# Grouped 1x1 convolution: a head of 136 columns in four pieces, the ring begun at column 104, and no unrolled tail

## The chip, the core and the metric

The kernel runs on one core of a Trainium2 chip. The metric is the device time of one execution in microseconds (us), as the median of several executions.

## The reference, cut to what matters

```python
H = W = 512; G = 4; Cg = 48; C = G * Cg; k = 1      # bf16
x: (1, H, W, C);  w: (k, k, G, Cg, Cg)
xg = x.reshape(B, H, W, G, Cg)
out = einsum('bhwgc,gcd->bhwgd', xg, w[0, 0])       # k = 1: no neighbours, no padding
return out.reshape(B, H, W, C)
```

Each of the 262,144 pixels has 192 channels in four groups of 48; each group is multiplied by its own 48x48 matrix. 100.66 MB are read and as much is written.

## The kernel before, in words

**Columns, groups, pairs.** A pixel's 192 channels are contiguous in memory. On the chip 128 pixels stand in 128 partitions; one such set is a *column* (384 bytes a partition). Four columns are a *group* (196.6 KB), two groups a *pair*. There are 2056 columns, 514 groups and 257 pairs. A group takes 12 steps on TensorE: six transposes (L350), which bring channels to the partitions, and six matmuls against the block-diagonal weights `wt` (L370). VectorE copies a pair's transposes from PSUM to SBUF (L409), ScalarE (ACT) casts a group's result from PSUM to SBUF (L446).

**Fields.** `plan_fields` cuts the columns into *fields*. In a full field every partition holds one contiguous run of pixels. Two fields of 48 columns are *partial*: they use 120 partitions and go in several DMAs, two on the hardware queue (SP for loads, ACT for stores) and three on POOL's queue (L296, L307; with tiny "fill" DMAs between them, L286). Each is followed by a field of 32 columns, and the two together fill one slot of the ring.

**The load ring.** `ring` has 240 columns in three slots of 80 (`BIG`). `plan_pieces` cuts full fields into loads of 80 columns, the first ones into those of `HEAD`. `Piece.at` is the place in the ring: here four times the group's number, modulo 240. SP issues the loads in order (L320); `freed(p)` says how many pairs must have been transposed (`t_done`) before a load may overwrite its place, which is 60 groups before its end.

**The store ring.** `oring` has 280 columns. `plan_stores` cuts the fields into stores: mostly at the grid `OGRID` (72, 140, 212, 280), and in the last field's last 240 columns into smaller ones. ACT walks through all 514 groups in a straight program. Ahead of the cast of group g it issues every store that ended before g-1, and then waits for the landing of the store that last used the place of group g:

```python
while todo and stores[todo[0]].g1 <= g - 1:
    issue(todo.pop(0))          # L442, DMA at L427
if over[g] is not None:
    landed(over[g])             # waits for the older store in this place
act.copy(out_columns(g)..., o_ps[...])   # L446
```

The PSUM result buffer `o_ps` holds two groups, so TensorE waits soon after ACT does.

**TensorE's program.** `step(pair)` transposes pair+1 and then multiplies pair. `plan_units` puts pieces together to *units* of 80 columns that fill a slot ("regular"); TensorE waits for a unit's load at its first group (L344), for a mixed unit (partial field plus 32 columns) for a semaphore that POOL raises when all its parts have landed (L299, L300). `loop_spans` finds the run of regular units, and how many rounds of 60 groups (30 pairs, the period of the ring) fit into it. Before: pairs 0 to 8 unrolled, 8 rounds of 30 pairs (9 to 248), pairs 249 to 256 unrolled. Loads of irregular units have semaphores of their own.

The stores and pieces around the end, before (columns, groups from and up to):

| store | columns | groups | place in oring |
|---|---|---|---|
| 21 | 72 | 350-368 | 0 |
| 22 | 48 | 368-380 | 72 |
| 23 (partial) | 48 | 380-392 | 120 |
| 24 | 32 | 392-400 | 168 |
| 25 | 80 | 400-420 | 200 |
| 26 | 72 | 420-438 | 0 |
| 27 | 68 | 438-455 | 72 |
| 28, 29, 30 | 40 each | 455-485 | 140, 180, 220 |
| 31 to 36 | 20, 28, 24, 20, 16, 8 | 485-514 | 260, then 0 on |

Of the kernel before, what the change touches and what calls it, by code (L numbers as in the profile page):

```python
# [24 lines left out]
BIG = 80  # L25
SLOTS = 3
RCOLS = SLOTS * BIG
OGRID = (72, 140, 212, 280)
OCOLS = OGRID[-1]
HEAD = (8, 24, 48)  # L30
LATE_COLS = 240
LATE_PART = 40
LAST_PARTS = (24, 20, 16, 8)
# [13 lines left out]

FILL_ROWS = 5
FILL_BEFORE = (2, 3)


class Field:


    def __init__(self, cols, blocks, g0, pix):
        self.cols, self.g0, self.g1 = cols, g0, g0 + cols // 4
        self.full = blocks is FULL
        self.blocks = []
        for (queue, r0, rows, outer, less) in blocks:
            self.blocks.append((queue, r0, rows, outer, pix, cols - less))  # L60
            pix += rows * (cols - less)
        self.pix_end = pix
        assert cols % 4 == 0


class Piece:

    def __init__(self, i, field, c0, size):
        self.i, self.field = i, field
        self.c0, self.c1, self.size = c0, c0 + size, size  # L70
        self.g0, self.g1 = field.g0 + self.c0 // 4, field.g0 + self.c1 // 4
        self.at = 4 * self.g0 % RCOLS
        self.full, self.blocks = field.full, field.blocks
        assert size % 4 == 0 and self.at + size <= RCOLS

# [8 lines left out]
def plan_fields(npix):  # L84

    parts, head = [], sum(HEAD)
    for slots, special in FRONT:
# [14 lines left out]
def plan_pieces(fields):  # L102
    pieces = []
    for f in fields:
        first = [f.cols]
        if f.full:
            first = list(HEAD) if not f.g0 and sum(HEAD) <= f.cols else []
        c = 0
        while c < f.cols:
            n = first.pop(0) if first else min(BIG, f.cols - c)  # L110
            pieces.append(Piece(len(pieces), f, c, n))
            c += n
    return pieces
# [27 lines left out]
class Unit:  # L141


    def __init__(self, pieces):
        self.pieces, self.g0, self.g1 = pieces, pieces[0].g0, pieces[-1].g1
        self.slot = pieces[0].at // BIG
        self.regular = pieces[0].at % BIG == 0 and 4 * (self.g1 - self.g0) == BIG


def plan_units(pieces):  # L150
    units, rest = [], list(pieces)
    while rest:
        n = 1
        if rest[0].g0 and rest[0].at % BIG == 0:
            while n < len(rest) and rest[n].at % BIG:
                n += 1
        units.append(Unit(rest[:n]))
        rest = rest[n:]
    return units
# [19 lines left out]
def bass_standalone__grouped__vision_kernel(nc, x, w, out):  # L179
# [6 lines left out]
    pieces = plan_pieces(fields)  # L186
    stores = plan_stores(fields)
    units = plan_units(pieces)
    unit_of = {g: u for u in units for g in range(u.g0, u.g1)}
    store_of = {g: s for s in stores for g in range(s.g0, s.g1)}  # L190
# [12 lines left out]
    def transfers(ap, tile, part, queues):  # L203
        f, c0, c1, at = part.field, part.c0, part.c1, part.at
        for n, (queue, r0, rows, outer, pix, cols) in enumerate(f.blocks):
            if queue not in queues:
                continue
            px = ap[pix:pix + rows * cols, :]
            if f.full:
                view = px.rearrange("(p i) n -> p (i n)", p=rows)[:, c0 * C:c1 * C]  # L210
            else:
                assert (c0, c1) == (0, f.cols)
                view = px.rearrange("(c a i) n -> a c (i n)", a=outer, c=rows // outer)
            yield n, view, tile[r0:r0 + rows, at * C:(at + (c1 - c0 if f.full else cols)) * C]
# [12 lines left out]
    with ExitStack() as es:  # L227
# [25 lines left out]
        fill_sem = [sem(f"fill{k}") for k in range(4 * len(mixed))]  # L253

        def columns(g):
            at = 4 * g % RCOLS
            return ring[:, at * C:(at + 4) * C]

        def out_columns(g):
# [9 lines left out]
        def _(gp):  # L269
# [12 lines left out]
            def filler():  # L282
                k = len(used)
                src = xf[0:2 * FILL_ROWS, 0:4].rearrange("(t p) n -> p t n", t=2)
                dst = fill[:, 8 * k:8 * k + 8].rearrange("p (t n) -> p t n", t=2)
                gp.dma_start(dst, src).then_inc(fill_sem[k], 16)  # L286
                used.append(k)

            for nth, u in enumerate(mixed):
                part = [p for p in u.pieces if not p.full]  # L290
                for p in part:
                    gp.wait_ge(t_done, freed(p))
                    for n, dram, sbuf in transfers(xf, ring, p, ("pool",)):
                        if n in FILL_BEFORE:
                            filler()
# [6 lines left out]
                for i, s in enumerate(stores):  # L302
                    if any(s.field is p.field for p in part):
                        for n, dram, sbuf in transfers(of, oring, s, ("pool",)):
                            if n in FILL_BEFORE:
                                filler()
# [16 lines left out]
        def _(pe):  # L323
# [12 lines left out]
            def transposes(pair):  # L336
                todo = []
                for g in groups(pair):
                    u = unit_of[g]
                    if g % 2 and pair:  # L340
                        pe.wait_ge(e_done[(pair - 1) % NTOK], 1)
                    if g == u.g0:
                        for key in unit_keys[u]:
                            pe.wait_ge(ld_sem[key], 16)  # L344
                        todo += unit_keys[u] if u.regular else []
                    xg = columns(g)
                    for ul in range(2):
                        for tc in range(3):
                            j = ul * 3 + tc
                            last = pe.transpose(xT_ps[:, g % NXP, j * 128:(j + 1) * 128],  # L350
                                                xg[:, j * 128:(j + 1) * 128], ident[:])
                            if todo and 0 < j < 5:
                                last.then_inc(ld_sem[todo.pop(0)], -16)
                assert not todo
                last.then_inc(t_done, 1)
# [125 lines left out]
```

## Time and profile before

| | |
|---|---|
| median of 8 runs | 478.5 us (477.38 to 482.52) |
| profiled execution | 477.61 us, of which span 475.8 us |
| moved by DMA | 201.57 MB, 424 GB/s over the span |
| busy: PE, weight loads, ACT, DVE | 430.9, 389.1, 388.4, 246.8 us |
| TensorE clock, mean granted | 0.974 |
| ACT idle, of it waiting for a store to land | 81.7 us, 19.7 us in 10 waits |
| last load issued, landed | 410.6 us, 434.6 us |
| last cast begins, last store issued | 470.05 us, 470.88 us |

The span runs from the first to the last instruction on the core. Loads are on queue q1 (SP), stores on q10 (ACT), POOL's DMAs on q0. A DMA's row gives the time from its issue to its landing, which includes its time behind others in the queue.

### The profile page before, as it was taken

How to read it: one execution, taken by the hardware profiler on the slowest of the kernel's cores; microseconds unless marked ns; L12 is line 12 of the kernel's file. 1: busy time of each engine (PE TensorE's matmuls, PEld its weight loads, DVE VectorE, ACT ScalarE, POOL GpSimd, SP SyncE). 2: the span in 40 equal slices, each digit the busy share in tenths (PEclk: the TensorE clock that was granted, in tenths of full speed). 3: DMA queues.
4: the chain of work that ended last, by engine and by line, in shares of the span. 5: the costliest groups of instructions: out<-in, count | busy, mean ns of one | idle time of the engine just before them, and what ended most of it. 6: DMA issues, size and time to landing. Idle time of an engine off the chain costs nothing.

```text
span 475.8 us, 13580 instructions
## 1 busy us (share of the span) xinstructions
PE 430.9 (91%) x6178; PEld 389.1 (82%) x6178; DVE 246.8 (52%) x258; ACT 388.4 (82%) x515; POOL 12.5 (3%) x28
## 2 busy tenths in 40 slices
PE   5999999999598999999998997899978998997994
PEld 5888888888597988888987896788867987886883
DVE  2655556555255555555554554455535554653552
ACT  2998899988477898999986886789858987885885
POOL 1000000200002000000000000200002000000000
PEclk9999999999889999999998999999989999997998
DMA  8999999999999999999999999999999999999997
GB/s 329 444 394 427 424 426 430 436 426 434 437 428 429 433 425 429 438 432 425 431 438 433 429 437 420 435 426 439 428 429 429 434 430 426 432 431 433 422 408 310
DMA packets 10674, 201.57 MB, mean 424 GB/s; under 512 B 2112, under 2 KB 2112, under 8 KB 2752
## 3 DMA queue, kind: packets, MB, share of 16 engines
q1 hardware_dynamic: 4320, 97.44, 48.0%
q10 hardware_dynamic: 5120, 97.42, 47.9%
q0 software_dynamic: 1216, 6.49, 3.3%
q8 instruction: 9, 0.15, 0.1%
q14 instruction: 9, 0.07, 0.0%
HBM read 100.68 MB, written 100.66 MB: 423 GB/s over the span
## 4 chain that ended last, share of the span: by engine, by line
DMA 50%; PE 40%; ACT 7%; issue 1%; ACTq 1%; SPq 0%; POOLq 0%
DMA out_dram<-oring 40%; PE o_ps L370 23%; PE xT_ps L350 17%; DMA ring<-in_x_dram 9%; ACT oring L446 7%; ACTq L427 1%; SPq L320 0%; SPq L313 0%; ACTq L420 0%; POOLq L300 0%; POOLq L299 0%; ACTq L429 0%
## 5 line engine op out<-in xcount | busy, mean ns | idle before, releaser
L446 ACT CAST oring<-o_ps 128x768 bf16<-128x768 f32 x514 | 387.1, 801 | 81.7 <-PE o_ps L370 56.0
L409 DVE COPY xT_sb<-xT_ps 128x1536 bf16<-128x1536 bf16 x257 | 246.1, 958 | 218.0 <-PE xT_ps L350 218.0
L370 PE MATMUL o_ps<-wt,xT_sb 128*128 128x144 bf16 (+1 forms) x3084 | 288.9, 236 | 27.9 <-ACT oring L446 22.2
L370 PEld LDWEIGHTS o_ps<-wt,xT_sb 128*128 128x128 bf16 x3084 | 212.4, 99 | 66.5 <-ACT oring L446 57.4
L350 PE MATMUL xT_ps<-ident,ring 128*128 128x128 bf16 x3084 | 222.1, 222 | 8.2 <-POOLq L300 4.9
L350 PEld LDWEIGHTS xT_ps<-ident,ring 128*128 128x128 bf16 x3084 | 189.9, 100 | 11.2 <-POOLq L300 5.1
L286 POOL DMA_DIRECT2D fill<-in_x_dram x8 | 4.6, 573 | 351.1 <-PE xT_ps L350 230.6
L296 POOL DMA_DIRECT2D ring<-in_x_dram x6 | 3.3, 560 | 0.0
L307 POOL DMA_DIRECT2D out_dram<-oring x6 | 3.3, 556 | 0.0
L332 PE MATMUL o_ps<-w_sb,esel 48*128 48x48 bf16 x10 | 0.6, 209 | 2.6 <-DMA w_sb<-in_w_dram 2.6
L332 PEld LDWEIGHTS o_ps<-w_sb,esel 48*128 48x128 bf16 x10 | 0.4, 111 | 2.6 <-POOL esel L273 2.6
L402 DVE CAST wt<-o_ps 128x480 bf16<-128x480 f32 x1 | 0.7, 658 | 3.2 <-PE o_ps L332 3.2
L446 ACT ACT_TABLE_LOAD x1 | 1.3, 1283 | 0.8 <-PEq L466 0.8
L273 POOL TENSOR_SCALAR_AFFINE_SELECT esel<-esel 48x272 bf16<-48x272 bf16 x1 | 0.4, 402 | 0.0
L270 POOL MEMSET esel<- 48x272 bf16 x1 | 0.3, 318 | 0.3 <-POOLq L466 0.3
L277 POOL TENSOR_SCALAR_AFFINE_SELECT ident<-ident 128x128 bf16<-128x128 bf16 x1 | 0.3, 282 | 0.0
L271 POOL MEMSET ident<- 128x128 bf16 x1 | 0.2, 198 | 0.0
L466 POOL MEMSET const-float32-0.0<- 128x1 f32 x1 | 0.1, 99 | 0.3 <-issue 0.3
L466 POOL MEMSET const-bfloat16-1.0<- 128x1 bf16 x1 | 0.1, 102 | 0.0
L466 POOL MEMSET const-uint8-127<- 128x1 uint8 x1 | 0.1, 102 | 0.0
L466 POOL MEMSET const-float32-1.0<- 128x1 f32 x1 | 0.1, 99 | 0.0
## 6 DMA issues: line engine op xcount, KB each, us to landing
ring<-in_x_dram SPq DMA_DIRECT2D x22, 3840.0 KB, 26.2
out_dram<-oring ACTq DMA_DIRECT2D x11, 3456.0 KB, 39.7
out_dram<-oring ACTq DMA_DIRECT2D x10, 3264.0 KB, 39.9
out_dram<-oring ACTq DMA_DIRECT2D x3, 1920.0 KB, 18.2
out_dram<-oring ACTq DMA_DIRECT2D x1, 3840.0 KB, 46.3
ring<-in_x_dram SPq DMA_DIRECT2D x2, 1536.0 KB, 33.1
out_dram<-oring ACTq DMA_DIRECT2D x2, 1536.0 KB, 41.9
out_dram<-oring ACTq DMA_DIRECT2D x1, 2880.0 KB, 37.5
```

Source lines behind the costliest of these rows:

```text
L273: gp.affine_select(out=esel[:], in_=esel[:], pattern=[[-1, ECOLS]], compare_op=AluOpType.is_equal, fill=0.0, base=ESHIFT, channel_multipli ...
L286: gp.dma_start(dst, src).then_inc(fill_sem[k], 16)
L296: gp.dma_start(sbuf, dram).then_inc(ld_sem[ld_key[p.i, n]], 16)
L307: gp.dma_start(dram, sbuf).then_inc(st_sem[i][n], 16)
L332: last = pe.matmul(o_ps[:, NOB - 1, col:col + CG], lhsT=esel[:, s0:s0 + 128], rhs=w_sb[:, g, :], start=True, stop=True, skip_group_check=True)
L350: last = pe.transpose(xT_ps[:, g % NXP, j * 128:(j + 1) * 128], xg[:, j * 128:(j + 1) * 128], ident[:])
L370: last = pe.matmul(o_ps[:, v % NOB, c0_:c1_], lhsT=xs[:, j * 128:(j + 1) * 128], rhs=wt[:, WOFF[tc]:WOFF[tc] + (c1_ - c0_)], start=(tc == ...
L402: dve.tensor_copy(wt[:], o_ps[:, NOB - 1, 0:WCOLS]).then_inc(wc_sem, 1)
L409: dve.tensor_copy(xT_sb[pair % NXS][:, 0:n * 2 * UC].rearrange("p (g c) -> p g c", g=n), xT_ps[:, b0:b0 + n, 0:2 * UC]).then_inc(e_done[pa ...
L427: act.dma_start(dram, sbuf).then_inc(st_sem[i][n], 16)
L446: act.copy(out_columns(g).rearrange("p (u c) -> p u c", u=2), o_ps[:, v % NOB:v % NOB + 2, 0:UC]).then_inc(fa_done[g % (2 * NTOK)] if g < ...
L466: nc = _bacc.Bacc("TRN2", target_bir_lowering=False, num_devices=1)
```

## The change: what it does

`HEAD` becomes (8, 24, 48, 56), 136 columns in four loads. `ring_at` shifts all places in the ring by the head: the head begins at column 104 and ends at 240, and the 80-column units begin at column 0 behind it. The head's 56 columns are kept out of the regular units (`g0 > 0`, and `plan_units` merges only behind the head). Group numbers and places of the output are given by the same rules as before, so these follow:

- The first field has 616 instead of 560 columns, the last one 400 instead of 456. The partial fields are groups 154 to 165 and 394 to 405 instead of 140 to 151 and 380 to 391.
- The loads are 8, 24, 48, 56 and then 80 columns, with the two mixed slots as before; the last load has 80 columns instead of 56. Up to the head's end and one slot more, 216 columns need no wait, where it was 240. The loads of 80 columns end at groups 54, 74, 94 and so on (514 the last) instead of 60, 80, 100 (500, then 514).
- The loop has 8 rounds of 30 pairs, as before, but pairs 16 to 255. Pairs 0 to 15 are unrolled ahead of it, and behind it only pair 256 (its matmuls).
- There are 38 stores instead of 37. From group 193 to 368 and from group 420 on they are cut at the same groups and lie at the same places. Those between: 368-385 (68 columns at 72, store 22), 385-394 (36 at 140), 394-406 (partial, 48 at 176), 406-414 (32 at 224), 414-420 (24 at 256).

```diff
@@ -27,7 +27,7 @@
-HEAD = (8, 24, 48)
+HEAD = (8, 24, 48, 56)
@@ -47,6 +47,11 @@
+def ring_at(g):
+
+    return (4 * g - sum(HEAD)) % RCOLS
@@ -69,7 +74,7 @@
-        self.at = 4 * self.g0 % RCOLS
+        self.at = ring_at(self.g0)
@@ -144,14 +149,14 @@
-        self.regular = pieces[0].at % BIG == 0 and 4 * (self.g1 - self.g0) == BIG
+        self.regular = self.g0 > 0 and pieces[0].at % BIG == 0 and 4 * (self.g1 - self.g0) == BIG
...
-        if rest[0].g0 and rest[0].at % BIG == 0:
+        if 4 * rest[0].g0 >= sum(HEAD) and rest[0].at % BIG == 0:
@@ -253,7 +258,7 @@
-            at = 4 * g % RCOLS
+            at = ring_at(g)
```

## The prediction

> **What bounds the kernel now.** First the page's slices, then the chain of waits, then the groups. The core's 16 DMA engines are busy from the second slice to the last but one, and half of the chain that ended last is DMA:
>
> ```profile
> PEclk9999999999889999999998999999989999997998
> DMA  8999999999999999999999999999999999999997
> ...
> DMA 50%; PE 40%; ACT 7%; issue 1%; ACTq 1%; SPq 0%; POOLq 0%
> ...
> L446 ACT CAST oring<-o_ps 128x768 bf16<-128x768 f32 x514 | 387.1, 801 | 81.7 <-PE o_ps L370 56.0
> ```
>
> 201.57 MB in 475.8 us is 424 GB/s on average, and 430 to 435 GB/s in the 20 us windows between 100 and 440 us. So the middle moves bytes at a fixed rate, and a stall of TensorE there costs nothing in itself: in the window from 120 to 140 us PE is busy for 14.8 us of 20, and the DMA share is 1.01. What can be gained or lost lies where the DMA engines are not full, which is the end (windows of 4 us; the columns that matter are PE, the fourth busy time, ACT, and the last three: clock, DMA share, GB/s):
>
> ```profile
> 428.00:432.00 4.00, 1.16 (x19) 0.93 (x17) 1.43 (x2) 0.98 (x2) 0.00 (x0) 0.87 1.03 444
> 432.00:436.00 4.00, 4.00 (x34) 3.90 (x33) 0.96 (x1) 2.35 (x4) 0.00 (x0) 0.50 1.00 432
> ...
> 456.00:460.00 4.00, 3.76 (x59) 3.30 (x56) 1.92 (x2) 3.42 (x6) 0.00 (x0) 1.00 0.96 407
> 460.00:464.00 4.00, 3.97 (x59) 3.43 (x56) 2.35 (x3) 3.27 (x5) 0.00 (x0) 1.00 0.95 394
> 464.00:468.00 4.00, 3.76 (x56) 3.35 (x54) 2.41 (x3) 3.71 (x6) 0.00 (x0) 1.00 0.93 393
> 468.00:472.00 4.00, 1.32 (x15) 0.78 (x12) 0.02 (x1) 2.59 (x4) 0.00 (x0) 0.99 0.89 362
> 472.00:476.00 4.00, 0.00 (x0) 0.00 (x0) 0.00 (x0) 0.00 (x0) 0.00 (x0) 0.50 0.39 157
> ```
>
> From 456 us on the engines run out of work (about 3.5 us of them unused): the last loads have landed by 434.6 us (issued 410.6, 24.0 us), stores alone remain, and ACT produces them too late. Why it is late stands in ACT's timeline:
>
> ```profile
> 401.18 0.80 ACT L446 CAST oring<-o_ps 128x768 bf16<-128x768 f32 x1 [2.02 <-DMA out_dram<-oring]
> ...
> 431.02 1.50 ACT L446 CAST oring<-o_ps 128x768 bf16<-128x768 f32 x2 [3.38 <-DMA out_dram<-oring]
> 432.89 1.60 ACT L446 CAST oring<-o_ps 128x768 bf16<-128x768 f32 x2 [0.37 <-PE o_ps L370]
> 435.77 1.60 ACT L446 CAST oring<-o_ps 128x768 bf16<-128x768 f32 x2 [1.28 <-PE o_ps L370]
> ```
>
> 44 casts start from 431.02 us on, so this wait is that of group 514-44 = 470. Its place in oring still belongs to store 25 (80 columns, groups 400 to 419), issued at 384.62 us with 46.3 us to landing. The wait costs 3.38 us, and TensorE, idle meanwhile, then runs at half clock: the six groups 470 to 475 take 7.69 us (431.02 to 438.71) where the 32 groups from 438 to 469 ran at (427.64-401.18)/32 = 0.827 us each (427.64 is 431.02 less the wait; store 26, which ends before group 438, is issued right behind the cast of 401.18, so that one is group 438), so 2.7 us more. After that the last groups run freely: cast of group 476 at 438.71, of group 513 at 470.05, last store issued 470.88, landed 4.4 us later.
>
> **What the Trainium skill says.** "DMA: Bandwidth & Descriptors", section "Where 436 GB/s comes from", gives 435 GB/s as the ceiling of the fabric; the windows' 430 to 435 agree, so the middle has no reserve. The same page, section "Queues, rings and completion order", says that each DMA engine takes the queues with work in turn, packet by packet; the trace agrees roughly, with SP's load queue and ACT's store queue at 52.8% and 46.2% of the engines from 330 to 350 us, and POOL's queue taking 11.2% from 384.5 to 401 us. "TensorE: Matmul & The Clock Gate", Part 1, says that about 3.4 us of idle halve the clock and as much work restores it, against a free-running window. The trace agrees loosely: 0.50 after the wait of 3.38 us, but also after one of 2.45 us (at 254 us), and not after one of 3.35 us (at 288 us).
>
> **The change, part by part.**
>
> *Head.* The 8, 24 and 48 columns stay; the next load is 56 instead of 80 columns, and all later full loads move by 14 groups. Unwaited loads cover 216 instead of 240 columns, but the fifth 80-column load waits for 7 pairs instead of 10, some 3 x 1.65 = 5 us (two groups of 0.827 us a pair) earlier (22.99 us now). 216 columns are 10.6 MB, 25 us at 432 GB/s, so the load queue has work past that moment. Cost nothing, hidden by the load queue; if it ran empty, each us would cost one.
>
> *Loop and tail.* The loop still runs 8 rounds of 30 pairs, from pair 16 instead of 9; the unrolled pairs are 16 ahead and 1 behind, instead of 9 and 8. Instructions and waits per pair are the same, the unrolled total is 47 pairs both times. The trace shows no gap at an entry or exit of the loop: 3.3 us of "issue" in TensorE's weight loads all lie before 8 us. I take 0, with bounds of -1 and +1 us, well under a pair's 1.65 us; covered by ACT's lead at best.
>
> *Issues.* SP issues the same number of loads, ACT one store more (38 against 37, 0.34 us in its queue). POOL's partial loads and stores are the same DMAs, 14 groups later. Stall on the first mixed unit (4.9 us at 129 us now): again, some 11 us later; under full DMA queues, so 0.
>
> *End of the loads.* The last load is 80 instead of 56 columns, requested at the same 227 transposed pairs, the one before at 217 instead of 220. The bytes left in the queue are the same, so it lands near 434.6 us, at the latest 410.6 + 18 (80 columns at half of 432 GB/s) + a wait of some 5 us on ACT = 436 to 440. Group 494 is reached about 20 us after group 470, after 445 us. Cost 0.
>
> *Stores.* Here lies the difference. The store grid is the same from group 193 to 368 and from 420 on. Between, it is 68, 36, partial 48, 32 and 24 columns instead of 48, partial 48, 32 and 80. So:
> - Group 470 waits for the partial store of groups 394 to 405 instead of store 25. That goes out at about group 407, near 373 us, and the slowest of POOL's partial stores took 41 us now: 373+4+41 = 418 us, before 427. The wait of 3.38 us goes, and with it its 2.7 us of half clock. The 24-column piece that ends at group 420 is first waited for by group 484, at some 440 us against a landing near 431.
> - What is late next: group 438 waits for store 22. This ended at group 380 and landed at 345.43+55.7 = 401.1 us; it now ends at group 385. Stores through group 400 landed at 367.61+49.5 = 417.1 us, so 0.8 us a group, and five groups add 4.0: 405.1 us. Against that, POOL's partial stores begin 12.7 us later (from 360 to 373), so that some 0.6 MB of the 1.6 MB that they moved by 401 us comes behind store 22 instead of ahead; half of it taken from ACT's queue (0.3 MB at its 150 GB/s from 373 to 401 us) is 2 us. I take 403.1 us, bounds 401.1 and 405.1. Group 438 could be cast at 399.2, so its wait grows from 2.0 to 3.9 us, and I charge the full 2.7 us of half clock for it.
>
> *Sum.* Without any wait after group 438, group 513 would be cast at 401.18+26.46+4.96+31.34 = 463.9 us. Plus 1.9 (store 22 later) plus 2.7 (half clock) is 468.5, against 470.05: **1.5 us earlier**. The end can follow that far: 2.35 + 13.61 MB moved after 434.6 us take 36.9 us at 432 GB/s, to 471.5, and a small transfer's fixed part (384 KB took 3.4 us on an empty queue, 0.9 of it data) puts the floor near 473 to 474, against 475.3: at most 1.3 to 3.8 us can be gained, say 2.5. The profiled execution took 477.61 us, span 475.8 and 1.8 around it, so 476.1 for it; the median is 0.9 higher, 478.5, so **477.0**.
>
> **The rivals.**
> *No half clock (0.20).* Store 22 lands by 402 us, the wait stays below 3 us and the clock at full: last cast near 465, and the DMA floor decides, 2.5 to 3.5 us earlier, 475.5. For it: waits of 2.0 and 2.1 us (401, 305 us) kept the clock. Against it: five more groups in that store.
> *Store 22 decides against it (0.22).* Groups 350, 368 and 380 landed at 365.7, 384.5 and 401.1: the last twelve at 1.38 us each. If that holds for 17 groups, store 22 lands at 384.5+23.5 = 408.0, 6.9 us later; with 2.7 the last cast is at 473.5, 3.5 us later than now, so 482.0. It turns from gain to loss where store 22 lands after 404.6, and exceeds 0.5% after 407. For it: the slope shown; against it: that slope lay under POOL's stores, which move back.
> *It does nothing that shows (0.13).* Fixed DMA rate, the same bytes, and waits that only change places: 478.5.
>
> **How the numbers follow.** 0.5% is 2.4 us, about what a measurement of this kernel can tell from no change. The main case has 0.45: 475.1 to 479.1 from the bounds of store 22 alone; of it I count 0.12 faster by over 0.5% and 0.33 within. No half clock: 0.17 and 0.03. Store 22 late: 0.20 slower, 0.02 within. Nothing: 0.09 within, 0.04 slower (the loop's bound of 1 us and scatter). Together faster 0.29, same 0.47, slower 0.24. The range, 475.0 to 481.5, leaves out about 0.08 below and 0.12 above.
>
> **What would show it.** Right: no wait of ACT on a store at group 470, a wait of 3 to 5 us at group 438 ending near 403 us with a clock of 0.5 after it, last cast near 468.5, DMA share above 0.95 until 468 us, loads done near 435 to 440, DMA share 1.0 in the middle. Wrong: another long wait after 440 us, a gap of TensorE at a loop boundary, DMA windows of the middle below 428 GB/s, or the load of group 494 waited for.

## The result, and the profile after

The changed kernel is **slower by 0.6%**: 481.44 us as the median of 20 runs (477.43 to 484.06) against 477.92 us for the kernel before (57 runs), a ratio of 1.0062 with a 95% interval of 1.0047 to 1.0078. I had forecast 477.0 us, 1.5 us below the 478.5 that I started from. The ratios in this document leave out runs that are over 1.5% above the fastest of their kernel as slow (two of tail_of_31, at 485.95 and 486.24 us, and one of before_second_late, at 484.35 us), and aren't the quotients of the medians. The profiled execution took 482.40 us, with a span of 480.7 us against 475.8.

The page, its slices and then the chain that ended last (the cast is line 451 now):

```profile
span 480.7 us, 13580 instructions
...
DMA  8999999999999999999999999999999999999995
GB/s 327 434 425 426 422 424 429 432 423 422 439 420 428 421 424 431 434 425 432 417 431 428 435 407 429 434 428 420 436 434 429 425 432 419 434 425 428 416 405 244
...
PE 47%; DMA 40%; ACT 9%; another core or an unknown queue 1%; issue 1%; ACTq 1%; SPq 0%; POOLq 0%
...
L451 ACT CAST oring<-o_ps 128x768 bf16<-128x768 f32 x514 | 387.3, 801 | 85.1 <-PE o_ps L375 57.0
```

Instruction counts and busy times are those of before to within 1 us. The DMA engines are as full as before up to the end, but the last slice falls to 5 tenths and 244 GB/s (before 7 tenths, as the prediction shows, and 310 GB/s). ACT's timeline around the wait that I had argued about:

```profile
407.01 0.80 ACT L451 CAST oring<-o_ps 128x768 bf16<-128x768 f32 x1 [2.03 <-DMA out_dram<-oring]
...
422.95 0.80 ACT L451 CAST oring<-o_ps 128x768 bf16<-128x768 f32 x1 [2.08 <-DMA out_dram<-oring]
...
473.68 0.80 ACT L451 CAST oring<-o_ps 128x768 bf16<-128x768 f32 x1 [0.21 <-issue]
```

The first is group 438 (the store that ends before it is issued at 407.04), the second group 455 (store 28, which ends there, is issued at 422.98), the third group 513. The wait of group 470 is gone, as predicted. Group 438 goes at 407.0 us, where I had 403.1. A wait that I had not foreseen follows at group 455, and behind it TensorE's clock falls (0.61 from 424 to 428 us; behind group 438 it stayed at 1.00). The last cast is 3.6 us later than before, not 1.5 us earlier. The delay is there before group 438: that group goes 5.8 us later than before, and from it to group 513 the changed kernel takes 66.7 us where the kernel before took 68.9. It builds up early. ACT waited for stores three times up to group 280 (groups 244, 263 and 280), where before it waited once, for 2.45 us, and cast group 280 at 254.56 us:

```profile
223.63 1.50 ACT L451 CAST oring<-o_ps 128x768 bf16<-128x768 f32 x2 [1.55 <-DMA out_dram<-oring]
...
241.19 0.80 ACT L451 CAST oring<-o_ps 128x768 bf16<-128x768 f32 x1 [1.84 <-DMA out_dram<-oring]
...
258.75 0.80 ACT L451 CAST oring<-o_ps 128x768 bf16<-128x768 f32 x1 [3.69 <-DMA out_dram<-oring]
```

The stores that groups 438 and 455 waited for, in the DMA rows of the stretches 355 to 360 us (store 22, issued at 357.87) and 365 to 370 us (store 23, issued at 367.90); the last number is us to landing:

```profile
out_dram<-oring ACTq DMA_DIRECT2D x1, 3264.0 KB, 49.1
...
out_dram<-oring ACTq DMA_DIRECT2D x1, 1728.0 KB, 55.0
```

So store 22 lands at 406.9 us and store 23 at 422.9. And the end (PE, fourth busy time ACT, then clock, DMA share, GB/s):

```profile
464.00:468.00 4.00, 3.86 (x56) 3.22 (x54) 2.65 (x3) 3.27 (x6) 0.00 (x0) 1.00 0.92 388
468.00:472.00 4.00, 3.66 (x54) 3.18 (x52) 2.06 (x3) 3.71 (x6) 0.00 (x0) 1.00 0.81 340
472.00:476.00 4.00, 1.16 (x12) 0.78 (x12) 0.00 (x0) 2.21 (x3) 0.00 (x0) 1.00 0.82 335
476.00:480.00 4.00, 0.00 (x0) 0.00 (x0) 0.00 (x0) 0.00 (x0) 0.00 (x0) 0.51 0.31 126
```

**Where the time went.** The Trainium skill, "DMA: Bandwidth & Descriptors", section "Why a DMA increments its semaphore by 16 and not by 1", says that a DMA runs on up to 16 engines that finish independently, that the semaphore counts them, and that only the full count means landed. The traces hold all 16 of these landings for each DMA over 128 partitions, so one can see how far the last engine is behind the median one; "lag" below is this distance. Worked out from the landing events (times from the span's start, us):

```
                               before                     changed
store that ends at        median  last   lag        median  last   lag
group 228                  252.3  254.5    2.1       253.9  258.7    4.7
group 280                  303.3  305.4    2.1       302.8  308.7    5.9
group 350                  364.5  365.7    1.2       363.2  371.2    8.0
380 / 385 (store 22)       397.4  401.1    3.7       393.6  406.9   13.4
400 / 394 (24 / 23)        412.4  417.1    4.7       408.9  422.9   14.0
group 465                  450.6  452.0    1.4       452.5  457.7    5.2
group 514 (last)           473.8  475.3    1.5       477.4  480.2    2.7
```

In stores 22 and 23 fifteen engines of the changed kernel are about where those of before are (their second-last landings are at 400.7 and 416.7 us): store 22 had landed in the median engine at 393.6 us, long before group 438 came at 405.0. One engine is 13 to 14 us behind, and the ring of stores waits for it. It isn't one engine alone all the time: from 440 to 470 us the last three landings are 5.2, 3.9 and 2.4 us behind the median (1.3, 1.1 and 0.8 before). Of the 4.9 us that the span grew, 3.7 are that the last store's median landing came later, as the last cast did, and 1.2 are its longer lag: in this execution the lag seems to have cost most by holding compute.

### The profile page after: what moved, and what is told of

It reads as the page before. It is cut to its first block, busy times and chain, and to the rows that moved or that the text cites. A ratio compares the mean times of both kernels' runs of the same rounds, so it can differ in the third digit from the quotient of the medians.

```text
span 480.7 us, 13580 instructions
## 1 busy us (share of the span) xinstructions
PE 431.5 (90%) x6178; PEld 390.0 (81%) x6178; DVE 246.7 (51%) x258; ACT 388.6 (81%) x515; POOL 12.5 (3%) x28
## 4 chain that ended last, share of the span: by engine, by line
PE 47%; DMA 40%; ACT 9%; another core or an unknown queue 1%; issue 1%; ACTq 1%; SPq 0%; POOLq 0%
DMA out_dram<-oring 30%; PE o_ps L375 27%; PE xT_ps L355 20%; DMA ring<-in_x_dram 9%; ACT oring L451 9%; ACTq L432 1%; SPq L325 0%; SPq L318 0%; ACTq L425 0%; POOLq L305 0%; POOLq L304 0%; ACTq L434 0%
```

## The experiments

The experiments are compared with the kernel before on the same chip. "Lag" is the distance of the last landing from the median one in the profiled execution, as a mean over all DMAs with 16 landings that landed from 180 us on, and over those that landed from 440 to 470 us.

| run | median us | ratio to before (95%) | profiled us | lag, mean | lag, 440-470 |
|---|---|---|---|---|---|
| before | 477.92 | 1 | 477.61 | 2.3 | 1.3 |
| changed | 481.44 | 1.0062 (1.0047 to 1.0078) | 482.40 | 4.8 | 5.2 |
| changed_again | 480.16 | 1.0049 (1.0029 to 1.0070) | 481.69 | 4.5 | 5.3 |
| head_both_early | 482.72 | 1.0100 (1.0076 to 1.0123) | 482.91 | 4.4 | 6.3 |
| head_first_early | 483.13 | 1.0100 (1.0073 to 1.0127) | 486.22 | 4.4 | 6.8 |
| before_first_late | 477.78 | 0.9995 (0.9983 to 1.0007) | 478.35 | 2.4 | 1.4 |
| before_second_late | 479.00 | 1.0040 (1.0016 to 1.0063) | 482.87 | 3.5 | 4.4 |
| last_load_24_56 | 480.73 | 1.0071 (1.0048 to 1.0094) | 479.71 | 3.4 | 4.0 |
| tail_of_31 | 481.63 | 1.0061 (1.0042 to 1.0079) | 482.86 | 4.3 | 5.3 |
| head160_five_pieces | 478.18 | 1.0003 (0.9988 to 1.0017) | 478.64 | 3.0 | 2.8 |
| head96 | 478.78 | 1.0002 (0.9986 to 1.0017) | 479.70 | 2.5 | 2.0 |
| head136_other_pieces | 478.94 | 1.0030 (1.0014 to 1.0045) | 477.88 | 2.2 | 1.5 |
| head136_other_no_tail | 478.45 | 1.0008 (0.9995 to 1.0020) | 477.94 | 2.5 | 0.7 |
| head_8_72_56 | 478.78 | 1.0009 (0.9995 to 1.0023) | 479.09 | 2.8 | 2.8 |
| head_8_24_24_80 | 479.81 | 1.0035 (1.0021 to 1.0050) | 481.04 | 3.6 | 4.2 |

**The place of the partial fields.** My first theory was that the partial fields, which come 14 groups later, cost the time. In the changed kernel, one slot earlier for both, or for the first alone:

```diff
-FRONT = ((6, ((48, PARTIAL), (32, FULL))), (11, ((48, UNEVEN), (32, FULL))))
+FRONT = ((5, ((48, PARTIAL), (32, FULL))), (11, ((48, UNEVEN), (32, FULL))))   # head_both_early
+FRONT = ((5, ((48, PARTIAL), (32, FULL))), (12, ((48, UNEVEN), (32, FULL))))   # head_first_early
```

> The changed kernel with its head, ring, loop (16 + 8x30 + 1 pairs) and 80-column last load as they are, but both pairs of partial field and 32-column field one slot (20 groups) earlier: groups 134 and 374 (changed kernel 154 and 394, before 140 and 380). Theory P (it is the later place of the partial fields that costs): back to 477 to 478.5 us. Rival H (head, ring phase, loop or last load cost it): stays at 480.5 to 482 us. Rival T (the wait on a store that ends at group 394, just ahead of the partial one, costs it): no such wait here, near 479 us.

> The changed kernel with only the first partial field one slot earlier (134 instead of 154), the second at 394 as in the changed kernel; a store ends at 394 and is waited for at group 449. Theory P: part of the loss comes back, 478.5 to 480 us. Rival T: 480.5 to 482 us. Rival H: 480.5 to 482 us.

And in the kernel before, one slot later for the first alone, or for the second alone:

```diff
+FRONT = ((7, ((48, PARTIAL), (32, FULL))), (10, ((48, UNEVEN), (32, FULL))))   # before_first_late
+FRONT = ((6, ((48, PARTIAL), (32, FULL))), (12, ((48, UNEVEN), (32, FULL))))   # before_second_late
```

> The kernel before with its head and loop, with only the first partial field moved one slot later (group 160 instead of 140; the second stays at 380, and all stores from group 315 on are those of the kernel before). Theory P: slower than before by 2 to 4 us (480 to 482), landings some 4 us late by group 200. Rivals H and T: 478 us, as before.

> The kernel before with only the second partial field one slot later (400 instead of 380; the first stays at 140). The stores around it are cut as in the changed kernel: group 438 waits for one ending at 385, group 455 for one ending at 400. Theory P: slower by 1 to 3 us, from the middle on. Rival T: slower by 1 to 3 us, but only by waits after group 438, landings before that as in the kernel before. Rival H: 478 us.

The theory fell as a whole: earlier fields made the changed kernel no faster (1.0100 twice), and a later first field does nothing to the kernel before. Rival T, the wait on a store that ends just ahead of the partial one, isn't enough either: it expected head_both_early near 479 us, and that took 482.72. A later second field does cost 0.4%, with a lag of 4.4 us and the head of before, so a head in four loads isn't the only way into the lag. Its profile shows how the lag reaches ACT, at groups 438 and 455:

```profile
405.23 0.80 ACT L446 CAST oring<-o_ps 128x768 bf16<-128x768 f32 x1 [7.18 <-DMA out_dram<-oring]
...
424.96 0.80 ACT L446 CAST oring<-o_ps 128x768 bf16<-128x768 f32 x1 [4.55 <-DMA out_dram<-oring]
```

ACT stands for those 12 us, and later the engines have too little to do (DMA share 0.51 from 460 to 464 us, 0.79 and less after it). So a lag can cost in two ways: the last engine ends alone, or compute is held by it and comes late for all. This execution took 482.87 us; the 17 of this kernel took 477.2 to 484.4 us.

**Loop, ring and last load.** Next: the loop's position and the head's odd pieces without a shift of the later loads; the last load asked for earlier; and another shift.

```diff
+HEAD = (8, 24, 48, 56, 24)      # head160_five_pieces, with FRONT's first 6 made 5
+HEAD = (8, 24, 64)              # head96
+HEAD = (8, 48, 80)              # head136_other_pieces
+            if f is fields[-1] and f.cols - c == BIG:       # last_load_24_56
+                first = [24, 56]
...
+                if part:
                     gp.wait_ge(go_sem, nth + 1)
```

> The changed code with HEAD = (8, 24, 48, 56, 24), 160 columns, and the first full run one slot shorter. The fields, all stores, and all loads from group 40 on are then those of the kernel before (partial fields at 140 and 380, last load 56 columns); what stays of the change is the odd 56-column piece in the head, the turned ring, and another loop: pairs 0 to 18 unrolled, 7 rounds, 28 pairs unrolled behind. Theory L (head pieces, ring places or the loop's position cost the time): 480.5 to 482 us, slow packets as in the changed kernel (some 5 us per DMA engine from 20 to 440 us). Theory S (the shift of the load boundaries against groups and fields costs it): 477.5 to 478.5 us, slow packets some 2.5 us as before.

> The changed kernel with its last load of 80 columns cut into 24 and 56, the 24 asked for at 220 transposed pairs instead of 227, as the kernel before asks for its last ones (TensorE still waits for both at group 494). If the late request of the last load costs time in the tail: 479.5 to 480.5 us. If not (load queue and waits on stores decide): 480.8 to 482 us.

> The changed code with HEAD = (8, 24, 64), 96 columns: loads end at groups 4 + 20k, partial fields at 144 and 384, the last load has 40 columns, loop from pair 11, 8 rounds, 6 pairs behind. Group 438 waits for a store that ends at 384, group 454 for the partial one at 384 to 395. Theory S with any shift harmful: 480 to 482 us, slow packets 4 to 5 us. Theory W (only the waits on stores around the second partial field count): 478.5 to 479.5 us, slow packets 2.5 to 3 us.

> The changed kernel with its 136-column head cut into 8, 48 and 80 columns instead of 8, 24, 48 and 56. Ring, fields and all later loads and stores are those of the changed kernel; the loop begins at pair 6 with 8 rounds, so that 11 pairs are unrolled behind it. Theory S: as the changed kernel, 480.5 to 482 us, slow packets some 5 us. Theory L (the cut of the head or the missing tail): back towards 478 to 479 us.

Ring places, the 56-column piece in itself and a loop of 7 rounds from pair 19 cost nothing (1.0003). The late request of the last load costs nothing either: asked for earlier, the kernel stays at 1.0071. Another shift (head96, with a head of three pieces) does no harm by its ratio (its median is 478.78 us beside 477.91), so a shift as such isn't it. But the same 136 columns in three pieces won back half of the loss, with all loads and stores from group 34 on unchanged. This run also had 11 pairs unrolled behind the loop, so the two had to be taken apart:

```diff
-            rounds = (run[-1].g1 - 2 * first - 2) // body        # tail_of_31
+            rounds = (run[-1].g1 - 2 * first - 2) // body - 1
-        self.regular = self.g0 > 0 and ...                       # head136_other_no_tail,
+        self.regular = 4 * self.g0 >= sum(HEAD) and ...          # with HEAD = (8, 48, 80)
```

> The changed kernel with 7 rounds of the loop instead of 8, so that pairs 226 to 256 are unrolled behind it; all loads, stores and places are those of the changed kernel. Theory L2 (a loop without an unrolled tail, or its position, costs the time; all four slow kernels so far had the loop from pair 16 to 255): back to 478 to 479 us. Theory E (one DMA engine falls behind the others, which the loop has nothing to do with): 480.5 to 482 us, with the last of the 16 landings of a store 8 to 14 us behind the median one near 400 us.

> The head of 8, 48 and 80 columns again, but with the loop of the changed kernel (pairs 16 to 255, one pair behind) instead of pairs 6 to 245. Theory L2: 481 to 482 us. Theory E with the cut of the head as what sets the engines apart: 478.5 to 479.5 us, as with the tail of 11 pairs.

> The changed kernel itself, unaltered. Theory E: its time goes with the lag of the last engine; where the profiled execution takes 478 to 479 us, the largest distance of the last landing from the median one stays under 10 us and its mean under 3 us; at 481 us and more it is 12 us or more and its mean over 4 us. Rival D (the DMA engines are all slower by the same): the same small distances at any time.

So the loop isn't what costs: 31 pairs behind it leave the loss where it was (1.0061), and with pieces of 8, 48 and 80 the loop without a tail takes no more than the kernel before, 1.0008. All that the change does except the cut of its head is in that kernel. (The same head with 11 pairs behind the loop had 1.0030; the two intervals overlap, so whether that loop costs a little isn't shown.)

The changed kernel run again was profiled at 481.69 us. Its last cast begins at 470.54 us, within 0.5 us of the kernel before, and still the end is late. The DMA share in its last windows shows the lag without any counting of landings:

```profile
468.00:472.00 4.00, 1.75 (x18) 1.17 (x18) 0.52 (x1) 3.08 (x5) 0.00 (x0) 0.94 0.91 381
472.00:476.00 4.00, 0.00 (x0) 0.00 (x0) 0.00 (x0) 0.00 (x0) 0.00 (x0) 0.50 0.58 235
476.00:480.00 4.00, 0.00 (x0) 0.00 (x0) 0.00 (x0) 0.00 (x0) 0.00 (x0) 0.50 0.05 22
```

From 476 to 480 us the share is 0.05: on average less than one engine of 16 (0.06) is moving bytes. With the other cut of the head (head136_other_no_tail) the same windows read

```profile
468.00:472.00 4.00, 0.00 (x0) 0.00 (x0) 0.00 (x0) 0.22 (x1) 0.00 (x0) 0.54 0.95 399
472.00:476.00 4.00, 0.00 (x0) 0.00 (x0) 0.00 (x0) 0.00 (x0) 0.00 (x0) 0.50 0.50 205
```

and all is over at 476.2 us: the last landing of the last store is 0.7 us behind the median one. Packets were on average no faster there: from 20 to 440 us each engine lost 3.9 us to packets longer than the median of their size, as in the changed kernel run again (3.8; 2.5 in the kernel before). So rival D falls as the whole cause: the engines drift apart. It isn't out as a part: the first profile of the changed kernel lost 5.0 us to such packets, and the slowest profile of all (head_first_early, 486.22 us) 5.4.

The same kernel shows what the prediction was worth without the lag. Group 438 waited for store 22, and the last cast came early:

```profile
402.98 0.80 ACT L451 CAST oring<-o_ps 128x768 bf16<-128x768 f32 x1 [3.64 <-DMA out_dram<-oring]
...
467.42 0.80 ACT L451 CAST oring<-o_ps 128x768 bf16<-128x768 f32 x1 [0.22 <-issue]
```

I had forecast 403.1 us, a wait of 3.9 us and a last cast at 468.5. No wait for a store followed at groups 455 or 470. Yet the last store landed at 475.7 us, where it was 475.3 before: the store queue was still full (DMA share 0.99 from 440 to 468 us).

**What in the cut does it.**

```diff
+HEAD = (8, 24, 24, 80)     # head_8_24_24_80, loop from pair 16 as in the changed kernel
+HEAD = (8, 72, 56)         # head_8_72_56
```

> The changed kernel with its 136-column head cut into 8, 24, 24 and 80 columns; loop, ring, fields and all other loads and stores are those of the changed kernel. Two theories of what in the head drives the DMA engines apart. C56: the odd last piece of 56 columns ahead of the 80-column loads; then this is near 478.5 us, mean distance of last and median landing under 3 us. CN: the number of pieces (four small loads ahead instead of three); then this is near 481 us, distance over 4 us.

> The changed kernel with its head cut into 8, 72 and 56 columns, all else as in the changed kernel. C56: near 481 us, mean distance of last and median landing over 4 us. CN: near 478.5 us, distance under 3 us.

It isn't the 56-column piece: with it and three pieces the ratio is 1.0009. Four pieces cost 0.35 to 0.7% in each of four kernels with the fields and stores of the change (8, 24, 24, 80; the change itself, with two variants); three pieces cost 0.1% twice, which isn't clear of nothing, and 0.3% once. So the cut of the head is shown to matter; that the number of pieces decides isn't, for the 0.35% of 8, 24, 24, 80 and the 0.30% of 8, 48, 80 with a tail can't be told apart. Against a rule by number alone stands also head160_five_pieces, with five pieces and no loss, but other later loads. Why one more small load in the first 20 us leaves one engine 5 us behind at 450 us **stays open**. The lags grow slowly: from 60 to 110 us they are alike (means of 2.1 us for the DMAs over 128 partitions in the kernel before, in the changed one and with 8, 48 and 80 columns without a tail), from 180 to 330 us the means over all DMAs are 3.7 us in the changed kernel and 2.9 in it run again, against 1.8 before and 2.2 with 8, 48 and 80 columns; and the traces don't name the engine of a packet. That the lag makes the time is supported by the table (every profiled execution with less than 3 us in the last column took 477.6 to 479.7 us, every one with 4.2 or more took 481.0 to 486.2, and the one at 4.0 took 479.7), but the lag at the end is itself a part of the time, and no run took the lag away by itself.

## Why the prediction was wrong, point by point

- *"So the middle moves bytes at a fixed rate, and a stall of TensorE there costs nothing in itself."* Nearly true of the sum of the engines: 426, 427 and 429 GB/s in the three 100 us stretches from 100 to 400 us, against 432, 432 and 430. Still, that is 1.2 MB less in those 300 us, an estimated 2.8 us at 432 GB/s. It fails for the landings, on which compute waits. I treated the 16 engines as one queue and carried the landings of before over to the changed kernel up to group 368: they came 4.2 us later at group 228, 5.6 at 350 and 3.5 at 368. **This is the step that failed**, and the sign with it; the experiments lead it back to the term *Head*, which I had put at nothing (below). The lag could have been seen in the trace of before: stores 21, 22 and 24 landed 3.5, 3.7 and 4.7 us after their median engine, and the 32-column load that ends at group 400 even 10.0 us.
- *"Group 470 ... The wait of 3.38 us goes."* Right: from group 438 to 513 it took 66.7 us, where 65.4 follow from my numbers and 68.9 were measured before. *"What is late next: group 438 waits for store 22 ... I take 403.1 us."* The place was right, the time not: 406.9 us. From store 21's landing to store 22's it took 18.9 us, where my numbers gave 18.6; the whole row was late, and group 438 itself came at 405.0 instead of 399.2, so that its wait was 2.03 us, not 3.9, and no half clock followed it.
- *Group 455.* I named one replacement for the wait that went, and not the next store in the ring. Store 23 landed at 422.9 us and held group 455 for 2.08 us; the clock in the window from 424 to 428 us was 0.61. The last cast came at 473.7 instead of 468.5 us. Without the lag this wait did not come (head136_other_no_tail).
- *Loop, last load, first mixed unit at 0.* Right by tail_of_31, last_load_24_56 and before_first_late, as far as these can tell.
- *"Head ... Cost nothing, hidden by the load queue."* Here sat the loss: with the head in three loads and all else as in the change the ratio is 1.0008 or 1.0009, with its four loads 1.0049 to 1.0062, so this term cost some 2 to 2.6 us and not nothing (an estimate: 0.40 to 0.54% of 478 us). The load queue was indeed never empty (the load that I expected about 5 us earlier was issued at 18.59 instead of 22.99 us, with its forerunner in flight until 30.0), and the cost isn't a wait at the head: it shows some 200 us later, as the distance between engines. I had given this term no bounds.
- *The gain of 1.5 us* didn't come where the lag was absent either: head136_other_no_tail has the same store cuts and stays at 1.0008, between -0.2 and +1.0 us. There the casts came as forecast, so what failed in this case is *"The end can follow that far"*: 16.6 MB of stores were left at 434.6 us instead of the 16.0 of before, and the full queue moved them at 422 GB/s (440 to 468 us), not at 432.
- *The rival "Store 22 decides against it"* had the sign, and 482.0 us; it named a turn at 404.6 us and 408.0 for the landing. It came to that by POOL's stores standing ahead of store 22. With its median engine landed at 393.6 us, that isn't what held it, so the nearness of its numbers is luck.
- *Readings.* The 20 us windows of before go from 425 to 435 GB/s, not from 430, so windows below 428, which I named as a sign of being wrong, were there already. The load that waits for 7 pairs is the second of 80 columns, not the fifth. A floor at 473 to 474 us leaves 1.3 to 2.3 us to be gained; the 3.8 belong to 471.5.

## What to carry to other kernels

Where a long stream runs on all DMA engines at once, a buffer is free when the slowest engine has landed, so read the spread of a transfer's landings, or the DMA share of the last windows (a share near one sixteenth is one engine alone), and not only the mean rate. An edit of the first small transfers can be free where it stands and still cost half a per cent at the end, as it did here; test such a cut with two or three variants before the rest of the change is judged. Compute that ends earlier gains nothing while the store queue is still full, so price the end by the bytes that are left and the rate of that stretch. When a change moves a wait in a ring, follow the next two or three places of the ring, not only the one that is freed.

## What the runs showed of the hardware that was not expected

Engines with like shares of the same transfers drifted apart by up to 14.5 us (the landing of the changed kernel's store that ends at group 414) while the DMA share of the windows around it (404 to 440 us) was 0.92 to 1.06. The drift differed from one profile of the changed kernel to the other, and the times spread with it: the changed kernel took 477.4 to 484.1 us, the kernel with a head of 8, 48 and 80 columns and the same loop 477.1 to 480.6. From 20 to 440 us most load packets of 30,720 bytes took exactly 1138 ns (2629 of 2833 before, 2377 of 2790 in the changed kernel); 208 packets of all sizes were longer by over 50 ns than the median of their size in the kernel before, and 383 in the changed one.
